# A new order table for the first two batches of an attention and gated-MLP kernel

## The chip, the core and the metric

The kernel runs on one core of a Trainium2 chip. Its engines are named as in the profile: PE multiplies matrices, DVE and POOL work on elements, ACT evaluates functions and copies, and SP issues most of the DMAs. The metric is the time of one execution on the device in microseconds (us). It is not the span: the span is the stretch between the first and the last instruction in the trace, and the time is a little longer.

## What is computed

Eight batches of 576 positions. Windowed attention of 8 heads (half of them with a window of 32 positions, half with every fourth of the last 128) gives x with 512 columns. A gated layer follows, and then a layer that mixes positions:

```python
gate = 1.0 / (1.0 + np.exp(-gate_pre))      # gate_pre: a causal convolution of x, 5 taps
val = x @ w_val
x = gate * val @ w_mid                       # 512 columns
h = np.maximum(x @ w_in, 0.0)                # 1024 columns
u, v = h[..., :512], h[..., 512:]
v_n = (v - mu) / np.sqrt(var + 1e-06)        # over the columns of v
v_s = np.einsum('ts,bsd->btd', w_spatial, v_n) + b_spatial[None, :, None]
out = (u * v_s) @ w_out
```

## The kernel before

The 8 heads of a batch are taken in 4 pairs, numbered 0 to 3; "(1,2)" below is batch 1, pair 2. For each pair the steps are `a_scores` (PE writes `s_ps`), `a_max`, `a_exp`, `a_sum` (the softmax on `e_t`, by DVE, ACT and POOL), `a_trans`, `a_pv` (PE writes `o_ps` from `pt` and `vv_t`, ACT copies it to `xt`), `a_conv` (five products on DVE, into `tt`) and `a_tanh`. In batch 0 `a_trans` goes through PE (`t_ps`). In batches 1 and later DVE transposes into one tile `et`, and SP copies it by 16 small DMAs, `pt<-et`, into the one tile `pt`; `a_pv` of the pair reads `pt`, so the copies of a pair cannot begin before `a_pv` of the pair ahead has read it.

The layers are `val` (`val_ps`), `v` and `norm` (`v_ps`, `v_t`), `u` (`u_ps`), `sp` (`sp_ps`) and `out` (`out_ps`). In place of two products by w_mid and w_in, the kernel first multiplies the two weights: `fuse("wiv", e)` for the columns of v and `fuse("wiu", e)` for those of u (both write `w_ps`). The raw weights arrive as 64-bit floating point; `w_f32` turns them into 32-bit numbers by an ACT and four DVE instructions (`wm_f`, `wiv_f`, `wv_f`, `wiu_f`, `wo_f`). From batch 1 on, and in `v`, `u`, `sp` and `out` always, every operand is split into a high and a low part, and three products replace one: ACT makes the high part (`gh`, `wiu_h`), POOL or DVE the low one (`gl`, `wiu_l`, `wm_l`, `wsp_l`, `w_l`). `val` of batch 0 is done on 32-bit operands unsplit, 32 products in all. The small results on PE share four buffers, which come free when the tile has been evicted; raw pieces of `w_spatial`, of its bias and of `w_out` share four buffers.

What sets the order is a queue. Each step is a key, and each key has one or more numbers (one for each piece of the step); the queue hands out the piece with the smallest number next, and every engine executes its instructions in the order in which the pieces were handed out. All instructions are recorded by one helper, so the profile gives line 635 for each. Batch 3 and later take their numbers from `EVERY`, shifted by 74.5 for each batch; the start takes them from the table `EARLY`:

```python
    def times(key):
        if key in EARLY:
            return EARLY[key]
        name, b, *rest = key
        return [t + PERIOD * (b - START) for t in EVERY[(name, *rest)]]
```

The numbers order the pieces and do nothing else.

Of the kernel before, what the change touches and what calls it, by code (L numbers as in the profile page):

```python
# [61 lines left out]
def _swapped(b, x):  # L62
# [172 lines left out]
    ("a_exp", 0, 3): (33.69,),
    ("load_mask", 3): (33.84,),
    ("a_trans", 0, 2): (34.99, 38.62, 39.08, 39.51, 39.95,),
    ("fuse", "wiv", 1): (35.58, 37.69, 39.20, 40.13, 41.28, 42.34,),
    ("load_vv", 1, 1): (37.97,),
    ("a_tanh", 0, 0): (38.49,),  # L240
    ("a_conv", 0, 1): (39.78, 45.98, 47.46, 51.00, 58.32,),
    ("load_w", "wiu", 0): (39.90,),
    ("a_sum", 0, 3): (40.23, 40.72,),
    ("val", 0, 0, 0): (42.47, 44.17, 44.70, 49.21, 50.01, 50.49, 51.00,),
    ("a_trans", 0, 3): (43.00, 43.58, 43.86, 44.29, 44.73,),
    ("a_conv", 0, 2): (44.10, 45.23, 46.72, 48.20, 56.83,),
    ("load_w", "wiu", 1): (44.23,),
    ("a_max", 1, 0): (44.55, 51.74,),
    ("fuse", "wiv", 2): (45.23, 47.35, 48.28, 49.74, 52.45, 53.58,),
    ("w_f32", "wiu", 0): (46.82, 48.95, 50.38, 52.42, 54.93,),  # L250
    ("a_conv", 0, 3): (49.56, 54.19, 56.09, 57.58, 59.06,),
    ("val", 0, 2, 0): (50.67, 51.21, 51.74, 57.08, 59.80, 61.65, 67.12,),
    ("split_pair", "wm", 0): (50.88, 65.63, 65.63, 69.24,),
    ("w_f32", "wiu", 1): (51.41, 60.98, 62.33, 63.81, 67.47,),
    ("val", 0, 3, 0): (52.27, 52.81, 54.94, 55.48, 61.59, 63.48, 64.28,),
    ("split_pair", "wm", 1): (52.94, 70.03, 70.36, 72.71,),
    ("val", 0, 1, 1): (53.34, 53.87, 54.41, 57.61, 61.96, 63.14, 65.97, 82.59,),
    ("a_exp", 1, 0): (53.46,),
    ("val", 0, 1, 0): (56.01, 56.54, 58.15, 58.68, 66.42, 66.90, 67.89,),
    ("a_tanh", 0, 2): (57.69,),  # L260
    ("split_sp", 4): (58.28, 76.95, 88.17, 92.02, 93.34, 95.12,),
    ("split_pair", "wiu", 0): (58.85, 59.55, 59.95, 62.64,),
    ("a_scores", 1, 1): (59.21,),
    ("split_sp", 0): (59.38, 72.85,),
    ("a_sum", 1, 0): (60.17, 61.13,),
# [21 lines left out]
    ("a_sum", 1, 1): (77.85, 80.09,),
    ("load_w", "wo", 1): (78.93, 95.96,),
    ("split_pair", "wv", 0): (79.55, 87.45, 90.10, 100.85,),
    ("fuse", "wiu", 2): (79.96, 80.71, 81.41, 82.10, 83.00, 83.61,),  # L290
    ("split_sp", 1): (80.11, 81.20,),
    ("load_vv", 1, 2): (80.24,),
    ("a_trans", 1, 1): (81.27, 82.11, 86.50, 89.06, 91.62,),
# [1178 lines left out]
```

## Time and profile before

| | us |
|---|---|
| time, median of 3 runs | 658.89 (658.78 to 660.42) |
| the profiled execution, its own time | 659.71 |
| its span | 657.9 |
| PE busy | 635.6 |
| DVE busy | 455.8 |
| POOL busy | 309.0 |
| ACT busy | 305.1 |

The profiled execution is 0.82 above the median, and 1.81 longer than its span. The granted clock of PE is 1.00 in every stretch. An engine's busy time is the sum over the stretches in which it had an instruction at work, whatever that instruction was held up by inside.

### The profile page before, as it was taken

The page shows a single profiled execution, that of the slowest core. Times are in us where ns is not written, and L with a number is a line of the kernel's source. Part 1 is how long each engine was busy: PE and PEld are TensorE (multiplying, and loading weights), DVE is VectorE, ACT ScalarE, POOL GpSimd, SP SyncE. Part 2 cuts the span into 40 slices and gives each one's busy share as a digit, 9 for nine tenths or more (in the row PEclk, how much of TensorE's full clock was granted, in tenths as well). Part 3 has the DMA queues.
Part 4 walks back from the last instruction along what each step waited for, and adds up shares of the span by engine and source line. Part 5 has one row for each costly group of instructions (what it writes and reads, how often), then busy time and mean ns, then how long its engine had stood idle before and what let it go on. Part 6 is the DMA issues. An engine that isn't in the chain of part 4 may idle for free.

```text
span 657.9 us, 17770 instructions
## 1 busy us (share of the span) xinstructions
PE 635.6 (97%) x7248; PEld 585.6 (89%) x7248; DVE 455.8 (69%) x789; ACT 305.1 (46%) x702; POOL 309.0 (47%) x378
## 2 busy tenths in 40 slices
PE   3889999999999999999999999999999999999998
PEld 2547789999899989999899989999899989999997
DVE  4999688997686588767676688767676688633410
ACT  4887676544443344443444434443444435442422
POOL 1114995746543374435634464435634364524430
PEclk9999999999999999999999999999999999999999
DMA  8971333352133332343123433343123411120002
GB/s 330 417 283 38 112 99 127 91 158 70 40 108 80 86 80 76 79 130 100 31 63 106 121 79 76 80 132 99 31 64 106 120 42 40 20 75 1 1 1 72
DMA packets 85605, 63.58 MB, mean 97 GB/s; under 512 B 64530, under 2 KB 74642, under 8 KB 85012
## 3 DMA queue, kind: packets, MB, share of 16 engines
q1 hardware_dynamic: 76308, 53.01, 28.3%
q10 hardware_dynamic: 9216, 9.44, 4.1%
q8 instruction: 57, 0.93, 0.6%
q14 instruction: 24, 0.20, 0.1%
HBM read 44.92 MB, written 9.44 MB: 83 GB/s over the span
## 4 chain that ended last, share of the span: by engine, by line
PE 80%; DVE 9%; DMA 4%; POOL 3%; ACT 3%; issue 1%; SPq 0%; ACTq 0%; DVEq 0%; POOLq 0%
PE sp_ps L635 17%; PE u_ps L635 14%; PE out_ps L635 14%; PE v_ps L635 14%; PE val_ps L635 13%; PE o_ps L635 4%; PE s_ps L635 3%; DVE tt L635 3%; DMA raw<-in_w_in 2%; DMA raw<-in_w_mid_t 1%; DVE wo_f L635 1%; DVE wiu_f L635 1%; POOL wsp_l L635 1%; ACT pt L635 1%; DMA qk_t<-in_qk 1%
## 5 line engine op out<-in xcount | busy, mean ns | idle before, releaser
L635 DVE SCALAR_TENSOR_TENSOR tt<-xt,cw,tt 128x576 f32<-128x576 f32 x116 | 118.6, 1029 | 1.2
L635 PE MATMUL sp_ps<-wsp_h,vh 128*128 128x288 f32 x320 | 93.7, 297 | 0.0
L635 POOL TENSOR_TENSOR gl<-tt,gh 128x288 fp32r<-128x288 f32 x64 | 61.1, 962 | 49.9 <-ACT gh L635 46.3
L635 POOL TENSOR_TENSOR g2l<-ru,g2h 128x288 fp32r<-128x288 f32 x64 | 55.6, 876 | 52.3 <-ACT g2h L635 52.2
L635 PE MATMUL u_ps<-gh,w_h 128*128 128x288 f32 x256 | 76.4, 298 | 0.0
L635 PE MATMUL out_ps<-g2h,wout_h 128*128 128x288 f32 x256 | 76.2, 298 | 0.0
L635 PE MATMUL out_ps<-g2h,wout_l 128*128 128x288 f32 x256 | 75.5, 295 | 0.2 <-POOL wout_l L635 0.2
L635 PE MATMUL u_ps<-gl,w_h 128*128 128x288 f32 x256 | 75.4, 295 | 0.0
L635 PE MATMUL sp_ps<-wsp_h,vl 128*128 128x288 f32 x256 | 75.4, 295 | 0.0
L635 PE MATMUL u_ps<-gh,w_l 128*128 128x288 f32 x256 | 75.4, 295 | 0.0
L635 PE MATMUL sp_ps<-wsp_l,vh 128*128 128x288 f32 x256 | 75.4, 295 | 0.0
L635 PE MATMUL out_ps<-g2l,wout_h 128*128 128x288 f32 x256 | 75.4, 294 | 0.0
L635 PE MATMUL val_ps<-xh,wval_h 128*128 128x288 f32 x224 | 66.8, 298 | 0.0
L635 PE MATMUL val_ps<-xl,wval_h 128*128 128x288 f32 x224 | 66.1, 295 | 0.7 <-POOL xl L635 0.7
L635 PE MATMUL val_ps<-xh,wval_l 128*128 128x288 f32 x224 | 66.0, 295 | 0.0
L635 POOL TENSOR_TENSOR xl<-xt,xh 128x576 fp32r<-128x576 f32 x28 | 42.5, 1518 | 47.2 <-ACT xh L635 46.0
L635 POOL TENSOR_TENSOR vl<-v_t,vh 128x512 fp32r<-128x512 f32 x32 | 41.9, 1311 | 41.6 <-ACT vh L635 41.6
L635 POOL TENSOR_TENSOR e_t<-e_t,sm 128x576 f32<-128x576 f32 x31 | 38.1, 1229 | 48.9 <-DVE sm L635 22.4
L635 PEld LDWEIGHTS sp_ps<-wsp_h,vh 128*128 128x128 f32 x320 | 60.0, 188 | 0.8
L635 PE MATMUL v_ps<-w_h,gh 128*128 128x512 f32 x160 | 58.8, 392 | 0.6 <-DVE tt L635 0.6
L635 PE MATMUL v_ps<-w_l,gh 128*128 128x512 f32 x160 | 58.5, 390 | 0.0
L635 ACT CAST g2h<-ru 128x288 fp32r<-128x288 f32 x64 | 27.2, 431 | 63.2 <-DVE ru L635 63.0
(127 smaller groups left out, 1644.4 us busy)
## 6 DMA issues: line engine op xcount, KB each, us to landing
qk_t<-in_qk SPq DMA_DIRECT2D x30, 592.0 KB, 4.4
vv_t<-in_vv SPq DMA_DIRECT2D x30, 384.0 KB, 3.6
out<-ob ACTq DMA_DIRECT2D x64, 144.0 KB, 1.8
raw<-in_w_in SPq DMA_DIRECT2D x4, 1024.0 KB, 4.9
pt<-et SPq DMA_DIRECT2D x240, 16.0 KB, 1.9
pt<-et SPq DMA_DIRECT2D x144, 20.0 KB, 2.7
raw<-in_w_mid_t SPq DMA_DIRECT2D x2, 1024.0 KB, 12.5
raw<-in_w_val SPq DMA_DIRECT2D x2, 1024.0 KB, 13.2
```

Of the source, the lines that this page charges most:

```text
L635: ins = self._tc.keep_in_program_order(fn(*args, **kwargs))
```

## The change

All 358 keys of `EARLY` stay, and the numbers up to about 153 are others. Those that follow, from `val` (1,1,1) on, are the same in both tables, and so are `EVERY`, `PERIOD` and `START`. No instruction is added or taken away: PE has the same 5424 matmuls, DVE the same 789 instructions. From the product `v` (1,0) on, the order on PE is the same in both. One key shows what the diff looks like:

```diff
-    ("a_pv", 1, 2): (105.11, 113.93, 115.39,),
+    ("a_pv", 1, 2): (104.156, 107.023, 113.475,),
```

On PE, the end of `val` of batch 0 (`val_ps` from `wv_f`) and the beginning of `fuse` for wiu. Before:

```order
L635 MATMUL val_ps<-xt,wv_f_441 128x288 x2
L635 MATMUL w_ps<-wiv_f_221,wm_f_156 128x512
L635 MATMUL o_ps<-pt,qkv 64x96 x12
L635 MATMUL w_ps<-wiv_f_221,wm_f_156 128x512 x2
L635 MATMUL val_ps<-xt,wv_f_441 128x288
L635 MATMUL w_ps<-wiv_f_221,wm_f_156 128x512
L635 MATMUL val_ps<-xt,wv_f_441 128x288 x16
L635 MATMUL s_ps<-qk_t 32x64 x36
L635 MATMUL val_ps<-xt,wv_f_441 128x288 x12
L635 MATMUL w_ps<-wiu_h,wm_h 128x512
```

And now:

```order
L635 MATMUL w_ps<-wiv_f_205,wm_f_137 128x512 x2
L635 MATMUL val_ps<-xt,wv_f_437 128x288 x2
L635 MATMUL o_ps<-pt,qkv 64x96 x12
L635 MATMUL s_ps<-qk_t 32x64 x36
L635 MATMUL val_ps<-xt,wv_f_437 128x288 x30
L635 MATMUL w_ps<-wiu_h,wm_h 128x512
```

The last four products of `fuse` for wiv and the scores of (1,1) now stand ahead of 30 products of `val` in a row. After them PE has, before, 6 products of wiu's fuse, the scores of (1,2), 12 of `v`, 27 of the fuse, `a_pv` of (1,0) and the last 15 of the fuse; now it has 6 of the fuse, 24 of `v`, 3 of the fuse, the scores of (1,2), `a_pv` of (1,0) and the last 39 of the fuse, and then 32 of `v` and 36 of `u`, the scores and `a_pv` of (1,1).

On SP, the copies of the pairs (1,2) and (1,3); a row with x4 is four issues. Before:

```order
L635 DMA pt<-et 32x192 x4
L635 DMA pt<-et 32x96 x4
L635 DMA pt<-et 32x192 x4
L635 DMA pt<-et 32x96 x4
L635 DMA mask_sb<-in_masks 128x576
L635 DMA qk_t<-in_qk 128x1184
L635 DMA vv_t<-in_vv 128x768
L635 DMA pt<-et 32x192 x4
L635 DMA pt<-et 32x96 x4
L635 DMA pt<-et 32x192 x4
L635 DMA pt<-et 32x96 x4
```

And now:

```order
L635 DMA pt<-et 32x192 x4
L635 DMA vv_t<-in_vv 128x768
L635 DMA pt<-et 32x96 x4
L635 DMA mask_sb<-in_masks 128x576
L635 DMA raw<-in_w_out 128x1024
L635 DMA pt<-et 32x192 x4
L635 DMA raw<-in_w_out 128x1024
L635 DMA pt<-et 32x96 x4
L635 DMA raw<-in_w_out 128x1024
L635 DMA pt<-et 32x192 x4
L635 DMA pt<-et 32x96 x4
```

Loads of `w_out`, of a mask and of `vv_t` now stand among the copies of (1,2), and those of (1,3) follow with one load of `w_out` between. The places of the two `a_pv` on PE have moved too: between `a_pv` of (1,1) and of (1,2) there are now 60 products of `u`, 38 of `sp` and the scores of (1,3), and between those of (1,2) and of (1,3) 72 of `sp`, 6 of `out`, 2 of `sp` and 6 of `out`.

## Rows read from the trace of the kernel before

**Rows 1.** The page: busy time of each engine, share of the span, instructions.

```profile
PE 635.6 (97%) x7248; PEld 585.6 (89%) x7248; DVE 455.8 (69%) x789; ACT 305.1 (46%) x702; POOL 309.0 (47%) x378
```

**Rows 2.** Busy us (instructions) of each engine by stretch, clock, DMA share, GB/s.

```profile
core 0: us, PE busy (x) PEld busy (x) DVE busy (x) ACT busy (x) POOL busy (x), PEclk, DMA share, GB/s
...
50.00:60.00 10.00, 10.00 (x108) 7.33 (x106) 10.00 (x15) 7.69 (x27) 1.40 (x1) 1.00 0.01 2
60.00:70.00 10.00, 8.88 (x104) 6.26 (x102) 9.97 (x16) 5.90 (x14) 9.40 (x7) 1.00 0.25 76
70.00:80.00 10.00, 9.67 (x53) 7.84 (x55) 7.17 (x13) 8.49 (x29) 9.86 (x9) 1.00 0.35 107
...
300.00:374.00 74.00, 74.00 (x890) 70.31 (x889) 52.38 (x95) 31.84 (x62) 35.68 (x47) 1.00 0.34 88
```

**Rows 3.** Waits of PE: for whom, us in total, times, longest.

```profile
PE s_ps L635 <- DMA qk_t<-in_qk: 8.3, 2, 4.9
```

**Rows 4.** Chain that ended last, its end: start, us, what.

```profile
588.99 12.72 PE val_ps L635 x96
601.71 12.72 PE v_ps L635 x56
```

**Rows 5.** PE in time: start, us, operation, count, idle before.

```profile
60.88 6.11 PE L635 MATMUL val_ps<-xt,wv_f 128*128 128x288 f32 x24 [0.85 <-DVE tt L635]
...
83.89 0.39 PE L635 MATMUL w_ps<-wiu_h,wm_l 128*128 128x512 f32 x1
...
107.63 0.98 PE L635 MATMUL s_ps<-qk_t 64*32 64x64 f32 x72 [1.07 <-DVE e_t L635]
...
115.87 1.21 PE L635 MATMUL o_ps<-pt,vv_t 128*64 128x96 f32 x24
...
131.17 1.21 PE L635 MATMUL o_ps<-pt,vv_t 128*64 128x96 f32 x24
```

**Rows 6.** DVE in time, 43 to 65 us: start, us, operation, count.

```profile
43.87 1.22 DVE L635 SCALAR_TENSOR_TENSOR wv_f<-raw,wv_f 128x1024 int32<-128x1024 int32 x1
...
45.00 0.52 DVE L635 TENSOR_SCALAR tt<-xt,cw 128x576 f32<-128x576 f32 x1
...
45.43 0.75 DVE L635 SCALAR_TENSOR_TENSOR e_t<-s_ps,mask_sb 128x576 f32<-128x576 f32 x1
...
46.10 3.73 DVE L635 SCALAR_TENSOR_TENSOR tt<-xt,cw,tt 128x576 f32<-128x576 f32 x5
...
50.77 0.46 DVE L635 SCALAR_TENSOR_TENSOR tt<-tt,val_ps 128x288 f32<-128x288 f32 x1
...
52.47 0.75 DVE L635 TENSOR_REDUCE mx<-e_t 128x9 f32<-128x576 f32 x1
...
54.26 0.69 DVE L635 SCALAR_TENSOR_TENSOR w_l<-w_ps,w_h 128x512 fp32r<-128x512 f32 x1
...
63.90 0.77 DVE L635 STREAM_TRANSPOSE et<-e_t 128x576 f32<-128x576 f32 x1
```

**Rows 7.** DMA issues of SP in time: start, us, count.

```profile
64.73 8.54 SPq L635 DMA_DIRECT2D pt<-et  x12
...
102.94 10.62 SPq L635 DMA_DIRECT2D pt<-et  x16
...
113.66 0.53 SPq L635 DMA_DIRECT2D mask_sb<-in_masks  x1
...
119.12 10.99 SPq L635 DMA_DIRECT2D pt<-et  x16
```

**Rows 8.** DVE and POOL by shape, 0 to 160 us: busy, mean ns, idle before.

```profile
L635 DVE SCALAR_TENSOR_TENSOR tt<-xt,cw,tt 128x576 f32<-128x576 f32 x21 | 18.8, 929 | 0.1
...
L635 DVE SCALAR_TENSOR_TENSOR tt<-tt,val_ps 128x288 f32<-128x288 f32 x15 | 6.6, 448 | 1.7 <-PE val_ps L635 1.7
...
L635 POOL TENSOR_TENSOR gl<-tt,gh 128x288 fp32r<-128x288 f32 x15 | 15.6, 1056 | 12.1 <-ACT gh L635 8.6 <-ACT xt L635 3.6
...
L635 POOL TENSOR_TENSOR wsp_l<-sp_raw,wsp_h 128x576 fp32r<-128x576 f32 x4 | 6.2, 1557 | 0.0
```

More of the change, by code (lines that the diff above doesn't have):

```diff
@@ L237 @@
[L237 to L265, printed above, removed]
@@ L287 @@
[L287 to L293, printed above, removed]
-    ("a_split", 1, 0): (81.34, 103.60,),
-    ("a_max", 1, 2): (82.10, 82.89,),
-    ("a_conv", 1, 1): (82.99, 98.42, 99.87, 102.15, 107.39, 108.75,),
@@ new lines @@
+    ("fuse", "wiv", 1): (11.208, 13.359, 22.199, 22.916, 26.739, 29.368,),
+    ("a_max", 0, 2): (11.447, 11.686,),
+    ("w_f32", "wiv", 1): (12.403, 16.465, 17.182, 17.421, 17.660,),
+    ("load_qk", 0, 3): (12.642,),
+    ("a_pv", 0, 3): (13.120, 36.297, 37.492,),
+    ("a_trans", 0, 1): (13.598, 14.075, 16.704, 18.615, 18.854,),
+    ("load_vv", 0, 0): (13.836,),
+    ("load_w", "wv", 1): (14.314,),
+    ("load_w", "wv", 0): (14.792,),
+    ("load_qk", 1, 0): (15.509,),
+    ("a_scores", 0, 3): (15.748,),
@@ new lines @@
+    ("a_exp", 0, 2): (16.226,),
+    ("fuse", "wiv", 3): (18.376, 20.766, 21.721, 22.677, 24.828, 28.890,),
+    ("w_f32", "wv", 1): (19.332, 28.412, 30.084, 31.518, 38.208,),
+    ("w_f32", "wv", 0): (19.571, 25.306, 25.545, 25.783, 30.323,),
+    ("a_sum", 0, 2): (20.049, 25.067,),
+    ("a_max", 0, 3): (20.288, 20.527,),
+    ("a_exp", 0, 3): (21.244,),
+    ("a_pv", 1, 0): (21.483, 64.014, 67.359,),
+    ("a_pv", 0, 1): (22.438, 23.872, 30.562,),
+    ("load_vv", 0, 1): (23.155,),
+    ("load_vv", 1, 0): (23.633,),
@@ new lines @@
+    ("load_mask", 2): (24.350,),
+    ("load_sp", 0): (26.022,),
+    ("a_sum", 0, 3): (26.261, 29.129,),
+    ("load_vv", 0, 2): (26.500,),
+    ("a_trans", 0, 2): (26.978, 27.695, 29.845, 30.801, 31.040,),
+    ("a_pv", 0, 2): (27.217, 31.757, 32.952,),
+    ("a_scores", 1, 0): (27.456,),
+    ("a_pv", 1, 1): (27.934, 90.536, 91.492,),
+    ("load_vv", 0, 3): (28.173,),
+    ("fuse", "wiv", 2): (28.651, 29.607, 32.235, 32.474, 35.102, 40.837,),
+    ("a_trans", 0, 3): (31.279, 31.996, 32.713, 33.191, 34.863,),
@@ new lines @@
+    ("w_f32", "wiu", 1): (51.828, 61.864, 62.341, 62.580, 64.253,),
+    ("split_pair", "wiu", 0): (52.306, 53.740, 55.412, 59.713,),
+    ("a_tanh", 0, 3): (53.023,),
+    ("a_max", 1, 1): (53.979, 59.952,),
+    ("val", 0, 3, 1): (54.695, 55.890, 56.368, 57.324, 58.757, 60.430, 76.678, 79.784,),
+    ("fuse", "wiu", 1): (57.563, 69.032, 70.704, 73.094, 77.395, 84.802,),
+    ("load_qk", 1, 2): (57.802,),
+    ("split_sp", 4): (58.518, 72.855, 80.740, 100.811, 102.006, 102.483,),
+    ("fuse", "wiu", 0): (59.235, 66.403, 70.226, 77.156, 77.634, 77.873,),
@@ new lines @@
+    ("out", 1, 1, 1): (213.790, 217.230, 220.810,),
+    ("val", 2, 0, 1): (215.390, 216.590, 217.180, 219.000, 219.510, 221.030,),
+    ("out", 1, 3, 1): (216.990, 220.000, 220.430,),
+    ("a_tanh", 2, 3): (218.410,),
+    ("a_pv", 3, 1): (218.450, 246.880, 247.320, 248.200, 249.900,),
+    ("a_scores", 3, 2): (218.980,),
+    ("val", 2, 0, 0): (220.030, 221.280, 221.880, 222.360, 222.870,),
+    ("val", 2, 1, 0): (221.680, 225.490, 226.380, 226.860, 227.370,),
+    ("val", 2, 2, 1): (222.880, 225.030, 226.750, 227.230, 228.270, 236.750,),
@@ L533 @@
+    ("a_split", 3, 3): (287.890, 288.640,),
+    ("out", 2, 3, 1): (289.080, 294.450, 294.880,),
+    ("a_tanh", 3, 3): (293.480,),
 }
```

602 lines of the change are left out of this document (293 added, 309 removed), and 19 rows, old and new, of the table EARLY.

## The prediction

> **What bounds the kernel now.** The busy times come first: PE works 635.6 us of a span of 657.9 [rows 1], so it idles 22 us in all. The stretches then say where. In a batch in the middle, 300 to 374 us, PE is busy 74.00 of 74 us [rows 2]: nothing is to be had there, and the changed table does not reach it. At the start PE waits 8.3 us for `qk_t` alone [rows 3], while the first inputs arrive; the new table loads that tile first as well. From about 14 us on DVE has no gap (10.00 of 10 us from 50 to 60, 9.97 from 60 to 70) and gets one only near 75 (7.17 from 70 to 80), while POOL goes from 1.40 to 9.40 and 9.86 [rows 2]. So up to some 75 us the order of DVE's work decides when PE can begin a product, and behind that PE itself is the bound, apart from single gaps such as the 1.07 us before the scores at 107.63 [rows 5].
>
> The orders on PE are equal from `v` (1,0) on. If PE has finished everything ahead of that product x us earlier, and nothing else is late, the whole rest moves up by x, because the rest is PE at work without gaps. So I look for x alone.
>
> For the walk I need PE's pace at work: 96 products of `val_ps` took 12.72 us, which is 0.1325 each (`u`, `sp` and `out` have the same shape), and 56 of `v_ps` 12.72, which is 0.227 each [rows 4]; those of wiu's fuse have the same 512 columns. A call of scores takes 0.98, an `a_pv` 1.21. A `val` product of batch 0 has two records, so the 24 records in 6.11 us are 12 products of 0.51 [rows 5].
>
> **The change part by part.** It adds and removes no instruction; each term below is a shift.
>
> *First, `val` of batch 0.* Its long row needs the fourth `wv_f`, which ended at 45.09 (43.87 + 1.22). In the new order DVE has more ahead of it: three convolution products (3 of the five that took 3.73, so 2.2), one eviction of scores (0.75), one maximum (0.75) and one scaling (0.52) [rows 6]. That is 4.2 us, so it ends at 49.3. What PE had between its pieces of `val` before is then done, and the row starts there. PE has four small buffers, so the fifth `val` tile, nine products later, waits until DVE has evicted the first one. Between that `wv_f` and that eviction DVE has six convolution products (4.5), one scaling (0.52), one `w_l` (0.69), one scaling of `wiu_f` (taken as long as that) and the eviction itself (0.46) [rows 6]: 6.9, so 56.2. Seventeen products are left: 17 x 0.49 to 0.51 is 8.3 to 8.7, and `val` ends at about 64.7. Before, it ended at 66.99 (60.88 + 6.11). That is 2.3 us earlier.
>
> *Second, wiu's fuse and `a_pv` of (1,0).* Behind `val` PE now has 6 + 24 + 3 products of 0.227 (7.5) and one call of scores (0.98), so it comes to `a_pv` (1,0) at 73.2. The copies `pt<-et` of that pair wait for DVE's transpose, which ended at 64.67 (63.90 + 0.77) [rows 6]. Summing the durations of all that stands ahead of it on DVE in either order gives 3.3 us less now: 61.4. Twelve copies took 8.54 us, 0.71 each [rows 7], so sixteen take 11.4, and a load of `qk_t` among them, taken as a mask's 0.53 [rows 7], makes it 73.3. From the end of the last copy's issue to `a_pv` it took 2.3 us in (1,2) (102.94 + 10.62 = 113.56; 115.87) and 1.06 in (1,3) (119.12 + 10.99 = 130.11; 131.17) [rows 5, 7]. So `a_pv` starts at 74.4 to 75.6, a wait of 1.2 to 2.4 that was not there before. Then 1.21 for it and 39 x 0.227 = 8.85: the fuse ends at 84.5 to 85.7. Before, it ended at 84.28 (83.89 + 0.39) [rows 5], but with 12 products of `v` fewer done, which are 2.7 us. With those it would have ended at 87.0, so the new order is ahead by 1.3 to 2.5. Against this stand the low parts: the last `wm_l` is 3.2 us further back in DVE's order, and the last `wiu_h` on ACT stands behind the copy of `a_pv` (1,0). I allow 0.9 for them at the low end: 0.4 to 2.5, and take 1.8, nearer to the bare walk, since the fuse's other products (27 of the 39) can run ahead of the last chunk's.
>
> *Third, the gap at 107.63.* The scores of (2,0) waited there until DVE had evicted those of (1,3) from the one tile `s_ps` (1.07 us [rows 5]). In the new order two `a_pv` and 86 products stand between these two calls, 2 x 1.21 + 11.4 = 13.8 us, in which DVE can do that eviction; I take +1.1, with 0 as the other bound.
>
> *Fourth, `a_pv` of (1,2) and (1,3).* `pt` is one tile, so a pair's copies begin after the `a_pv` ahead. Between (1,1) and (1,2) PE has 98 products of 0.1325 and one call of scores, 14.0 us. The copies need 10.6 to 11.0, the four loads among them some 2.1 (each as the mask's 0.53), and 1.06 to 2.3 pass from the last issue to `a_pv` [rows 5, 7]: 13.8 to 15.4, a wait of 0 to 1.4. Between (1,2) and (1,3) PE has 86 products, 11.4 us; the copies need 11.7 to 13.3, a wait of 0.3 to 1.9. Before, (1,3) came 14.1 us after (1,2) had ended (115.87 + 1.21; 131.17), and PE had work for all of it. Together 0.3 to 3.3; I take 1.5, a little under the middle.
>
> *The sum:* 1.8 + 1.1 - 1.5 = 1.4 us earlier, with 0.4 + 0 - 3.3 = -2.9 and 2.5 + 1.1 - 0.3 = +3.3 as bounds. The profiled execution took 659.71 (1.81 of it outside the span) and would take 658.3; the median stands 0.82 lower, so the time I give is **657.5**.
>
> [...] A convolution product, two inputs in SBUF, takes 0.75 us in a row of five at 46.10, when POOL is nearly idle, and 0.929 on average up to 160 us; an eviction of a `val` tile, one input in PSUM, takes 0.46 and 0.448, POOL busy or not [rows 6, 8]. [...]
>
> **The rivals.**
>
> *The copies take all of it (no change).* With both waits of the fourth term at their upper ends the sum is 1.8 + 1.1 - 3.3 = -0.4: 659.3. For it: 16 issues took 10.6 us or more in both rows of SP [rows 7]. Against it: only 1.06 us passed from the last issue to `a_pv` in the later one.
>
> *Slower: a load in front of the copies of (1,1).* On SP the fifth load into the four raw buffers now stands right before the copies of (1,1), and its buffer comes free when POOL has made a `wsp_l` (1.557 us [rows 8]), the fifteenth piece of POOL's work since its first `gl`. POOL's work ahead of it depends on ACT's last `wiu_h`, behind `a_pv` (1,0); by sums it ends near 82. Then 16 copies (10.6), two loads (1.1) and 1.06 to 2.3: 94.8 to 96.0. PE comes to `a_pv` (1,1) at about 98.1 (the fuse's end at 85.1, 32 x 0.227, 36 x 0.1325, 0.98). The slack is 2 to 3 us. It decides from the point where that `wsp_l` ends after 85; at 90 the wait is some 5 us, and the sum 1.4 - 5 = -3.6: 662.5. For it: POOL was busy 9.40 and 9.86 of 10 us there [rows 2]. Against it: the slack.
>
> [...]
>
> *More than the sum.* If the fuse loses nothing at all, the waits of the fourth term stay at their lower ends, and DVE meets less of POOL from 75 to 150 us, the gain is the upper bound of the sum or a little more, 3.3 to 4.2: 654.7 to 655.6. For it: PE still idles 1.5 us between 60 and 80 [rows 2]. Against it: it needs all three.
>
> **How the numbers follow.** What a measurement of this kernel tells from no change is about 0.3%, 2 us: faster is under 656.9, slower over 660.9. Chances: the sum as forecast (655.6 to 658.6) 0.45; more than that 0.17; the copies take it 0.12; POOL under the convolution 0.09; slower by the load or another such wait 0.17. Faster holds the second case and half of the first, 0.40; slower is the last, 0.17; same is the rest, 0.43. The likeliest case's own range is 655.6 to 658.6. For eight in ten I go from 654.5, the end of the larger gain, to 661.4, which leaves most of the last case out.
>
> **What would show it.** `val` of batch 0 ends near 64.7 in place of 66.99; PE waits 1 to 2 us before `a_pv` (1,0) and the fuse ends near 85 with 24 products of `v` done; no gap before the scores of (2,0); waits of about 0.4 and 1.1 before `a_pv` of (1,2) and (1,3); `v` (1,0) 1.4 us earlier. A wait before `a_pv` (1,1), a `val` row that ends after 66, or a wait of several us at a fuse would make the prediction wrong.

## The result, and the profile after

The changed kernel takes 663.17 us (median of 17 runs, 660.26 to 666.81), the kernel before 659.23 (17 runs beside them, 657.66 to 661.12). The ratio is 1.0058, 95% interval 1.0041 to 1.0075: slower by 0.58%. The prediction gave 657.5, most likely the same or faster, with a range up to 661.4; the time lies above it. The profiled execution took 666.81, the longest of the 17, 7.10 over that of before (659.71), so its waits and its clock are those of a long execution: its mean granted clock is 0.992, that of the median execution 0.995.

By the page, the span is 665.0 us, 7.1 more than before. PE is busy 2.3 us longer for the same work [rows 1] and stands still for 27.1 us, 4.8 more:

```profile
PE 637.9 (96%) x7248; PEld 590.1 (89%) x7248; DVE 456.8 (69%) x789; ACT 304.2 (46%) x702; POOL 307.4 (46%) x378
```

By stretches (columns as in [rows 2]):

```profile
30.00:40.00 10.00, 10.00 (x52) 4.67 (x56) 9.24 (x16) 6.52 (x23) 1.39 (x4) 0.83 0.46 176
60.00:70.00 10.00, 10.00 (x44) 7.96 (x43) 9.68 (x15) 7.40 (x20) 7.82 (x8) 1.00 0.28 79
70.00:80.00 10.00, 9.64 (x128) 7.72 (x127) 8.83 (x15) 5.97 (x19) 7.73 (x7) 1.00 0.06 14
...
110.00:120.00 10.00, 5.82 (x114) 5.09 (x112) 4.71 (x9) 5.01 (x21) 6.09 (x7) 1.00 0.54 159
...
150.00:160.00 10.00, 7.99 (x90) 7.64 (x88) 5.13 (x11) 0.73 (x2) 2.31 (x2) 1.00 0.34 93
160.00:170.00 10.00, 8.68 (x38) 8.19 (x39) 8.39 (x16) 4.92 (x11) 8.06 (x13) 0.66 0.40 92
...
300.00:374.00 74.00, 74.00 (x890) 70.32 (x890) 53.95 (x96) 31.72 (x62) 35.87 (x46) 1.00 0.30 80
```

From 60 to 70 us PE now has no gap (8.88 before [rows 2]); in its place it is busy 5.82 of 10 from 110 to 120 and 7.99 from 150 to 160. Two stretches have a granted clock under 1 (the first columns are the stretch, its length and PE's busy time, the third number from the end is the clock), where before had 1.00 throughout:

```profile
30.00:34.00 4.00, 4.00 (x6) 1.70 (x7) 3.77 (x7) 0.52 (x2) 1.23 (x3) 0.57 0.99 374
161.00:165.00 4.00, 3.68 (x15) 3.68 (x16) 2.56 (x7) 2.40 (x6) 3.23 (x8) 0.50 0.37 99
165.00:170.00 5.00, 5.00 (x25) 4.51 (x24) 4.83 (x9) 1.79 (x4) 4.84 (x6) 0.83 0.49 101
```

Read in windows of half a us, the clock is 0.50 from 30.5 to 33.5 us and from 160.0 to 166.5, and 1.00 in the others from 28 to 43 and from 160 to 175, save the three in which it changes (0.71, 0.88 and 0.76); so the stretches with a value between hold some of either. In PE's timeline (start, us, operation, idle before) there is a long idle stretch at each, of 2.46 and of 3.33 us; the clock falls 0.3 us behind the end of the first and 2.0 us into the second:

```profile
29.89 8.83 PE L635 MATMUL w_ps<-wiv_f,wm_f 128*128 128x512 f32 x16 [2.46 <-DVE wiv_f L635]
...
51.79 14.82 PE L635 MATMUL val_ps<-xt,wv_f 128*128 128x288 f32 x60
...
76.34 0.68 PE L635 MATMUL o_ps<-pt,vv_t 128*64 128x96 f32 x10 [0.36 <-DMA pt<-et]
...
85.74 0.39 PE L635 MATMUL w_ps<-wiu_h,wm_l 128*128 128x512 f32 x1
...
98.07 1.03 PE L635 MATMUL s_ps<-qk_t 64*32 64x64 f32 x72
99.03 1.41 PE L635 MATMUL o_ps<-pt,vv_t 128*64 128x96 f32 x24
...
113.53 0.40 PE L635 MATMUL sp_ps<-wsp_h,vh 128*128 128x288 f32 x1 [1.77 <-ACT ru L635]
...
115.58 0.97 PE L635 MATMUL s_ps<-qk_t 64*32 64x64 f32 x72
117.19 0.91 PE L635 MATMUL o_ps<-pt,vv_t 128*64 128x96 f32 x12 [0.64 <-DMA pt<-et]
119.87 0.84 PE L635 MATMUL o_ps<-pt,vv_t 128*64 128x96 f32 x12 [1.76 <-DMA pt<-et]
...
161.32 0.61 PE L635 MATMUL val_ps<-xh,wval_h 128*128 128x288 f32 x1 [3.33 <-DVE tt L635]
...
166.53 0.49 PE L635 MATMUL v_ps<-w_h,gh 128*128 128x512 f32 x1
```

These answer to [rows 5]. `val` of batch 0 ends at 66.61 (51.79 + 14.82; before 66.99), the fuse of wiu at 86.13 (85.74 + 0.39). The scores of (1,3) start at 98.07, right ahead of `a_pv` (1,1), and those of (2,0) at 115.58, without a gap; the call that the section on the change names between the two `a_pv` is that of (2,0). Ahead of it comes a wait of 1.77 us for ACT's `ru`, behind it both halves of `a_pv` (1,2) wait for the copies (0.64 and 1.76), and at `val` of batch 1 PE waits 3.33 us for DVE. That last place, shortly ahead of the point from which the two tables are equal, is called the join below. `v` (1,0) starts at 166.53; before it started at 158.52:

```profile
158.52 0.40 PE L635 MATMUL v_ps<-w_h,gh 128*128 128x512 f32 x1
```

To see where these 8.0 us arise although the orders on PE differ, I subtract from the start of a product the time of all PE work ahead of it at full pace (0.1325 for a `val`, 0.227 for a `v` as in [rows 4], 0.49 for a `val` of batch 0, and so on). What is left is the time that PE has lost so far: idle, at a lower clock, or in rows next to a stop (the first product behind the 1.77 us took 0.40 where the next ones took 0.29 or 0.30). The columns are points with equal work done.

| PE's lost us | at wiu's fuse | after 85 us of work | after 105 | after 127 | at `v` (1,0) | end |
|---|---|---|---|---|---|---|
| before | 21.65 | 25.27 | 25.66 | 26.99 | 27.01 | 33.90 |
| after | 21.17 | 22.77 | 28.46 | 29.11 | 35.02 | 40.97 |

So the new order was ahead as forecast, by 2.5 us after 85 us of work, and lost 5.7 by 105 (4.17 of it the three idle stretches from 111 to 120) and 5.9 by `v` (1,0). The second loss is 3.33 of idle time and 2.4 of clock: 21 products in 5.21 us (161.32 to 166.53) in place of 21 x 0.1325 = 2.8.

On SP, the copies of (1,2) (answering to [rows 7]):

```profile
100.25 0.33 SPq L635 DMA_DIRECT2D raw<-in_w_out  x1
100.63 1.43 SPq L635 DMA_DIRECT2D qk_t<-in_qk  x2
102.16 3.49 SPq L635 DMA_DIRECT2D pt<-et  x4
105.70 0.70 SPq L635 DMA_DIRECT2D vv_t<-in_vv  x1
106.44 4.22 SPq L635 DMA_DIRECT2D pt<-et  x4
110.77 1.20 SPq L635 DMA_DIRECT2D mask_sb<-in_masks  x1
112.07 0.38 SPq L635 DMA_DIRECT2D raw<-in_w_out  x1
112.50 2.42 SPq L635 DMA_DIRECT2D pt<-et  x4
115.02 0.53 SPq L635 DMA_DIRECT2D raw<-in_w_out  x1
115.59 2.42 SPq L635 DMA_DIRECT2D pt<-et  x4
```

They take 15.85 us (102.16 to 118.01), where [rows 7] has 10.62. The four loads among them are 2.8 of it; the first eight copies take 0.87 and 1.06 each, the last eight 0.60. On DVE this is handed on, since `et` and `pt` are single tiles and DVE works in order. Before, the transpose of (1,3) came without a wait:

```profile
118.32 0.77 DVE L635 STREAM_TRANSPOSE et<-e_t 128x576 f32<-128x576 f32 x1
```

And now:

```profile
103.59 3.96 DVE L635 TENSOR_SCALAR v_t<-v_t,mv,rs 128x512 f32<-128x512 f32 x1
...
120.27 0.78 DVE L635 STREAM_TRANSPOSE et<-e_t 128x576 f32<-128x576 f32 x1 [5.40 <-DMA pt<-et]
...
149.65 0.81 DVE L635 SCALAR_TENSOR_TENSOR tt<-tt,val_ps 128x288 f32<-128x288 f32 x2
...
156.95 0.78 DVE L635 STREAM_TRANSPOSE et<-e_t 128x576 f32<-128x576 f32 x1 [4.70 <-DMA pt<-et]
...
160.82 0.81 DVE L635 SCALAR_TENSOR_TENSOR tt<-tt,val_ps 128x288 f32<-128x288 f32 x2
```

The transpose of (1,3), at 120.27, waits 5.40 us, that of (2,1), at 156.95, 4.70, with evictions of `val` tiles behind it in the queue; PE's 3.33 us end with the first of them, at 160.82.

### The profile page after: what moved, and what is told of

Same layout as the page of the kernel before. It is cut to its first block, busy times and chain, and to the rows that moved or that the text cites. A ratio compares the mean times of both kernels' runs of the same rounds, so it can differ in the third digit from the quotient of the medians.

```text
span 665.0 us, 17772 instructions
## 1 busy us (share of the span) xinstructions
PE 637.9 (96%) x7248; PEld 590.1 (89%) x7248; DVE 456.8 (69%) x789; ACT 304.2 (46%) x702; POOL 307.4 (46%) x378
## 4 chain that ended last, share of the span: by engine, by line
PE 82%; DVE 8%; ACT 3%; DMA 3%; SPq 1%; issue 1%; POOL 1%; DVEq 0%; POOLq 0%; ACTq 0%
PE sp_ps L635 16%; PE out_ps L635 15%; PE val_ps L635 14%; PE u_ps L635 14%; PE v_ps L635 13%; PE o_ps L635 4%; PE s_ps L635 3%; PE w_ps L635 2%; DMA pt<-et 1%; SPq L635 1%; DVE wm_f L635 1%; DMA raw<-in_w_mid_t 1%; DVE wiv_f L635 1%; DVE wo_f L635 1%; DVE tt L635 1%
## 5 line engine op out<-in xcount | busy, mean ns | idle before, releaser
L635 DVE SCALAR_TENSOR_TENSOR tt<-xt,cw,tt 128x576 f32<-128x576 f32 x116 | 116.9, 1011 | 1.4
L635 POOL TENSOR_TENSOR gl<-tt,gh 128x288 fp32r<-128x288 f32 x64 | 59.4, 934 | 46.8 <-ACT gh L635 46.7
```

Source lines behind the costliest of these rows:

```text
L635: ins = self._tc.keep_in_program_order(fn(*args, **kwargs))
```

## Experiments

Every edit moves pieces in the queue's order, and no instruction is added or taken away. Each median is beside runs of the kernel before on the same chip, and the ratio is to them. "After" is the changed kernel. Three theories are tested. A: PE's start is really earlier, and the loss comes from about 100 us on, from loads among the copies and the single `et` and `pt`. B: DVE is held up by POOL there. C: the idle stretch at 27 us and the lower clock behind it make the loss. One execution of each kernel was profiled; the waits below are of that one.

**Two halves.** e1, e7 and e8 begin in after's order and go on in before's; e2 begins in before's and goes on in after's. The place where the two orders meet is called the seam.

```diff
 e1: after's order up to the last copy of (1,1)
 e7: after's order up to the fifth val tile of batch 0
 e8: as e7, with the edit of e5
-    then after's order
+    then the rest in before's order
 e2: before's order up to the last copy of (1,1)
-    then before's order
+    then the rest in after's order
```

> The new order up to the last copy of pair (1,1) into pt, and behind it the old order of whatever is left. All theories agree on the profile up to 90 us: as in the changed kernel, some 1 us ahead of the old one at the end of wiu's fuse. Theory A (the loss is made by the copies of (1,2) and what stands among them on SP, from 100 us on, and is handed on through the tile et to DVE at the join): not slower than before, 657 to 659.5. Theory B (DVE is held up by POOL from 100 us on, as in the 3.96 us scaling of v_t): the same, since that part is the old one. Theory C (the loss is made at the start, by the idle PE at 27 us and the lower clock after it): slower than before by 2 us or more, 661 to 663.

Measured: 671.61, ratio 1.0185 (1.0172 to 1.0198). PE waits 4.9 us ahead of an `a_pv` and 3.96 ahead of scores; neither wait is in before or in after. The seam makes them, so e1 says nothing of the front half.

> The counterpart: the old order up to the last copy of pair (1,1), and behind it the new order of whatever is left. Theories A and B: most of the loss is there, 661 to 664. Theory C: no loss, 658 to 660.

Measured: 661.13, ratio 1.0023 (1.0013 to 1.0034). Behind before's front, after's tail costs 0.23%, perhaps less: in the profiled execution 1.4 of the 2.2 us that PE is behind at `v` (1,0) are lost ahead of wiu's fuse, where the order is before's (an idle stretch of 1.72 us at 34 us, and a granted clock of 0.76 from 34 to 40). The only new wait is 2.66 us of `val` for DVE at the join. The copies of (1,2) have the same kinds of loads among them, but take 12.5 us, and `a_pv` (1,2) does not wait: there PE comes later, the first loads of `w_out` were issued at 81 and 88.5 us, and fewer loads stand right ahead.

> The new order up to the fifth val tile of batch 0, and behind it the old order of whatever is left: the cut lies ahead of everything that the copies of batch 1 depend on. If the new start is worth what its profile shows, 0.5 us at the end of val, with the lower clock in it, the time is that of before or up to 1 us less: 658 to 659.5. If the first cut's loss was in the start, it is slower by 2 us or more.

> The same with the two products of the fuse moved as in the run for the start. If the lower clock at 30 us costs what the products' length says (1.4 us), this is 1 to 2 us faster than before, 657 to 658.5, and the best so far; if the clock matters to nothing, it is the same as the run without it.

Measured: 661.88, ratio 1.0043 (1.0031 to 1.0056), and 661.35, ratio 1.0033 (1.0022 to 1.0044). Both have one large wait, 4.07 us for DVE's `wm_l` at about 71 us, again from the seam, with a clock of 0.50 in e7 and 0.72 in e8 from 70 to 76 us (several products behind the wait take 0.63 us, those from 77 us on 0.39 or 0.40), and no other over 0.6 from there to `v` (1,0): e7's lost time grows from 28.35 once that is over to 30.72 at `v` (1,0), with before's order. The front half alone could not be told apart from its seam. Nor does the pair price the clock at the start: there e7 has 1.96 us of idle time and the full clock, and e8, which was to mend it, 2.00 us and the lower clock.

**One part undone.** e3 puts DVE's transpose of (2,1), and four that follow it, behind a convolution product and two evictions of `val`; e4 takes loads out from among the copies; e5 moves two products of wiv's fuse (two records each); e6 moves POOL's work off the stretch from 104 to 117.

```diff
 e3, DVE
-L635 STREAM_TRANSPOSE et<-e_t 128x9x2x32
 L635 SCALAR_TENSOR_TENSOR tt<-tt,val_ps 128x288 x2
+L635 STREAM_TRANSPOSE et<-e_t 128x9x2x32
 e4, SP
-L635 DMA qk_t<-in_qk 128x1184 x2
 L635 DMA pt<-et 32x192 x4
+L635 DMA pt<-et 32x96 x4
+L635 DMA pt<-et 32x192 x4
+L635 DMA pt<-et 32x96 x4
 L635 DMA vv_t<-in_vv 128x768
+L635 DMA raw<-in_w_out 128x1024 x3
+L635 DMA qk_t<-in_qk 128x1184
 e5, PE
-L635 MATMUL w_ps<-wiv_f_205,wm_f_137 128x512 x4
+L635 MATMUL w_ps<-wiv_f_205,wm_f_137 128x512 x2
 ...
-L635 MATMUL w_ps<-wiv_f_205,wm_f_137 128x512 x8
+L635 MATMUL w_ps<-wiv_f_205,wm_f_137 128x512 x10
 e6, POOL
+L635 TENSOR_TENSOR e_t<-e_t,sm 128x576
 L635 TENSOR_TENSOR wval_l<-wv_f_437,wval_h 128x512 x2
-L635 TENSOR_TENSOR e_t<-e_t,sm 128x576
 L635 TENSOR_TENSOR xl<-xt,xh 128x576 x2
```

> The changed kernel with one step moved on DVE: the transpose of pair (2,1) and the four steps that need the tile it frees (the scores of (2,2) out of PSUM, their maximum, difference and exponential) stand behind the last product of the convolution of (1,3) and the evictions of two val tiles. Nothing else moves. If the transpose, which waits for the copies out of et, holds up PE at the join (theory A's last step), the wait of 3.3 us of val at 158 us and the lower clock behind it go: 3 to 5 us less than the changed kernel, 658 to 660. If val waits for something else there, no change: 662 to 664.

Measured: 665.9, ratio 1.0099 (1.0084 to 1.0113). The wait of `val` is gone, and one of `v_ps` stands in its place (who waits, for whom, us in total, times, longest):

```profile
PE v_ps L635 <- DVE tt L635: 3.7, 1, 3.7
```

> The changed kernel with the loads moved on SP: the first qk_t of batch 2 goes ahead, to behind the copies of (1,1); the second qk_t, vv_t of (1,3), three pieces of w_out and a mask go from among the copies of (1,2) to behind them. Two pieces of w_out's conversion follow their loads on ACT. Theory A: the copies of (1,2), 15.9 us from the first to the last issue, take 11 to 12, a_pv of (1,2) waits 2 us or more less, and the copies of (2,0) and the transpose of (2,1) come earlier by the same: 658 to 661. Theory B: the scaling of v_t still takes 4 us, DVE is as late, 662 to 664.

Measured: 661.83, ratio 1.0032 (1.0018 to 1.0046). The copies of (1,2) now run without a break, and `a_pv` (1,2) does not wait:

```profile
99.45 10.26 SPq L635 DMA_DIRECT2D pt<-et  x16
```

This is 0.64 a copy, and the ratio falls from 1.0058 to 1.0032, a difference that the two intervals just bear out. But `ru` (1.9), `a_pv` of (1,3) (1.1) and the join (2.3) still wait.

> The changed kernel with two products of wiv's fuse moved on PE: the second chunk's first two wait until the scores of (0,3) are done, so that PE has 1.85 us of work in the stretch at 27 us in which it idled 2.46 us for wiv_f. Nothing else moves. Theory C (the idle PE and the lower clock behind it, 0.83 from 30 to 40 us, cost 1 to 2 us at the start): the granted clock stays 1.00, the second half of the fuse takes 7.4 us in place of 8.8, and the time falls by 1 to 2 us, to 661 to 662. Theory A alone: the copies are as late whatever PE does before, within 0.5 us of the changed kernel.

Measured: 664.62, ratio 1.0076 (1.0064 to 1.0088). At the start the profiled execution does what it should:

```profile
29.03 7.13 PE L635 MATMUL w_ps<-wiv_f,wm_f 128*128 128x512 f32 x16 [1.04 <-DVE wiv_f L635]
```

The idle time falls from 2.46 to 1.04 us, the clock stays at 1.00, and the 16 records take 7.13 in place of 8.83. PE is 4.6 us ahead of before after 85 us of work (20.68 lost) and 0.7 behind after 105 (26.37). At wiu's fuse it was 2.9 ahead. The gain is gone 20 us of work later, with the same waits as in after, the lower clock at the join among them (0.66 from 156 to 166 us). Theory C fails: the start is mended, and the time is no shorter.

> The changed kernel with four of POOL's pieces moved behind the softmax product of (1,3): two wval_l and the two xl that take over their buffer. They are the pieces during which a scaling of v_t on DVE took 3.96 us. Theory B (DVE held up by POOL sets the end there): the scaling falls to 0.5 to 2 us, PE's wait of 1.8 us for ru at 112 us goes, and the time falls by 1.5 us or more, to 661.5 or less. Theory A (the copies of (1,2) set the end): ru's wait shrinks, but a_pv of (1,2) waits for the copies by as much more, and the time stays within 0.7 us of the changed kernel.

Measured: 665.95, ratio 1.009 (1.007 to 1.0109). The wait for `ru` is gone, so POOL's work in that stretch made it; `a_pv` (1,2) waits 2.58 and 1.09 instead. Theory B names a true wait, but taking it away wins nothing.

**Several parts undone together.** e9 mends the join further (the transpose of (2,1) also behind `xt`), e10 is e4 and e5, e11 is e10 with e6 and an earlier softmax sum of (2,0), e12 is e11 with e9.

```diff
 e9, DVE
-L635 STREAM_TRANSPOSE et<-e_t 128x9x2x32
 L635 SCALAR_TENSOR_TENSOR tt<-tt,val_ps 128x288 x2
 L635 TENSOR_TENSOR xt<-o_ps,xt 128x4x96
+L635 STREAM_TRANSPOSE et<-e_t 128x9x2x32
```

> The changed kernel with the join mended in one more step than the earlier run did: the transpose of (2,1) and its four followers stand behind the evictions of two val tiles and behind DVE's part of a_pv (2,0), and POOL's two clearings of xt for it stand ahead of two gl. If the wait at the join is only the place of these pieces on DVE, PE's waits at 158 to 165 us shrink to 1 us or less and the clock stays at 1.00: 4 to 6 us less than the changed kernel in its profile, about 659 to 660.5. If the join is late because the copies of (2,0) and (2,1) are late, the wait moves once more, to a_pv (2,1) near 172 us or to v (1,0): 662 to 666.

> The changed kernel with both the fuse's two products moved (as in the run for the start) and the loads moved (as in the run for the loads). Theory A: the start alone gave nothing because the copies of (1,2) held the end; with these mended its 2 to 3 us reach further, and the time falls by more than the loads alone gave: 659 to 661. If the join loses whatever comes, it stays at 661.5 to 663.

> The same and two more: POOL's four pieces moved as in the run for POOL (ru's wait at 112 us), and the softmax sums of (2,0) on DVE and POOL moved ahead of two pieces of w_out's conversion, so that the transpose of (2,0), which came 4.7 us later than before at 139 us, comes earlier. Theory A: the copies of (2,0) begin at 134 us or earlier (139.9 in the changed kernel, 135.2 before), the wait at the join is below 1.5 us, and the time is 656.5 to 659.

> The same and the mended join. If the join's wait is a matter of order on DVE alone, 0.5 to 2 us less than the run without it; if the copies set it, the copies of (2,1) now begin later than they need and it is 0 to 2 us more.

Measured: e9 664.28, ratio 1.0069 (1.0047 to 1.0092); e10 660.61, 1.0032 (1.0019 to 1.0045); e11 662.66, 1.0056 (1.0044 to 1.0068); e12 665.18, 1.009 (1.0077 to 1.0103). e9's wait goes to `v_ps` (2.5 us), and so does e12's. e10 has the ratio of e4 alone. In its profile the start was not mended, although the edit of e5 is in it:

```profile
29.32 8.83 PE L635 MATMUL w_ps<-wiv_f,wm_f 128*128 128x512 f32 x16 [2.02 <-DVE wiv_f L635]
```

e11 has 4.9 us less lost than before after 85 us of work, and then waits 2.10 for DVE's `ru`, 0.84 for `wout_l`, 1.21 for ACT's `ob` and 1.51 at the join, with a clock of 0.76 from 124 to 131 us: nothing is left.

**The opposite, and the late `w_out`.** e13 puts loads among the copies in the kernel before. In after, e14 splits `w_spatial` earlier, which frees the raw buffers, so that all four loads of `w_out` go ahead of the copies of (1,2). e15 is e14 and e5.

```diff
 e13, SP, against before
+L635 DMA qk_t<-in_qk 128x1184 x2
 L635 DMA pt<-et 32x192 x4
 L635 DMA pt<-et 32x96 x4
+L635 DMA vv_t<-in_vv 128x768
+L635 DMA raw<-in_w_out 128x1024
 L635 DMA pt<-et 32x192 x4
+L635 DMA mask_sb<-in_masks 128x576
+L635 DMA raw<-in_w_out 128x1024
 L635 DMA pt<-et 32x96 x4
 e14, SP, against after
+L635 DMA raw<-in_w_out 128x1024 x2
 L635 DMA qk_t<-in_qk 128x1184
+L635 DMA raw<-in_w_out 128x1024 x2
 ...
-L635 DMA raw<-in_w_out 128x1024
 L635 DMA pt<-et 32x192 x4
-L635 DMA raw<-in_w_out 128x1024
 L635 DMA pt<-et 32x96 x4
-L635 DMA raw<-in_w_out 128x1024
```

> The kernel before with one edit, the opposite of e4: two loads of qk_t go ahead of the copies of (1,2), and a load of vv_t, two of w_out and one of a mask among them; nothing else is moved. Theory A (loads ahead of and among these copies cost PE time, because et and pt are single tiles): a_pv of (1,2) waits about 2 to 4 us where it did not wait before, and the time is 1.5 to 4 us over that of before (ratio 1.002 to 1.006). Rival (the copies have slack, and the loss comes from the order of DVE's and POOL's work): under 1 us at a_pv of (1,2), ratio within 1.0015 of 1.

Measured: 667.97, ratio 1.0135 (1.0118 to 1.0152). `a_pv` (1,2) waits 7.0 us, where theory A gave 2 to 4:

```profile
PE o_ps L635 <- DMA mask_sb<-in_masks: 5.2, 1, 5.2
PE o_ps L635 <- DMA pt<-et: 1.8, 1, 1.8
```

On SP, ahead of the copies:

```profile
96.24 12.89 SPq L635 DMA_DIRECT2D qk_t<-in_qk  x2
```

This row says why: the second `qk_t` held SP until 109.13, just after the scores of (2,0) at 107.81, which free its buffer (from 95 us on SP waits 11.9 us for `s_ps`), so the copies began 6.3 us later than in [rows 7]. The direction holds, that what stands ahead of and among these copies is paid by PE; the size is mostly the wait for that buffer, and not the issue of loads. So e13 does not show what loads among the copies cost by themselves.

> The changed kernel with the splitting of w_spatial (ACT's wsp_h, POOL's wsp_l) some 40 pieces earlier, so that the raw buffers come free sooner, and the four loads of w_out ahead of the copies of (1,2) in place of one ahead and three among them. Theory A (late w_out loads among the copies are the root): the copies of (1,2) take under 12 us, the scaling of v_t is not held 4 us by POOL, a_pv of (1,2) and (1,3) wait under 1 us together, and the time falls by 2 to 3 us from the 663.2 of the changed kernel. Rival (the loads then block SP ahead of the copies, waiting for their buffers): the copies of (1,2) begin 2 us or more later, a_pv waits as long or longer, and nothing is won.

> The edit of e14 and that of e5 (two products of wiv's fuse behind the scores of (0,3), which took the long idle stretch at 27 us away) together on the changed kernel. Theory A: the 3 us that e5 won at the start are kept as far as about 125 us, the wait at the join (val_ps, some 2 to 3 us) stays, and the time is 658 to 661, at or a little over that of before. Rival (each won us turns into a wait on the next late piece, whatever the order of the loads): 661 to 664, with new waits of 2 us or more between 100 and 130 us.

Measured: 663.75, ratio 1.0069 (1.0051 to 1.0087), and 664.0, ratio 1.0071 (1.0048 to 1.0094). In both, `a_pv` (1,2) waits only 0.25 us, and between 85 and 105 us of work 2.6 and 2.55 us are lost in place of 5.7. The time does not fall: two new waits for POOL stand at 87 and 93 us, and the join still waits, 3.29 us in e14 and 2.14 in e15. In e15's profile the start is not mended either (2.03 us idle and the lower clock). The waits of e14:

```profile
PE val_ps L635 <- DVE tt L635: 3.3, 1, 3.3
...
PE v_ps L635 <- POOL gh L635: 1.1, 1, 1.1
PE v_ps L635 <- POOL gl L635: 1.1, 1, 1.1
```

Theory A's claim that these loads are the root of the loss fails here; that they make the waits of `a_pv` holds.

**The join.** e16 moves the softmax sums of (2,0) ahead of an eviction on DVE and of three pieces on POOL, and one load of `qk_t` behind four copies; e17 is e14 with it, e18 is e15 with it.

```diff
 e16, POOL
+L635 TENSOR_TENSOR e_t<-e_t,sm 128x576
 L635 TENSOR_TENSOR wout_l<-wo_f_1532,wout_h 128x512
 L635 TENSOR_TENSOR g2l<-ru,g2h 128x288
 L635 MEMSET pt 128x1152
 L635 TENSOR_TENSOR wout_l<-wo_f_1670,wout_h 128x512
-L635 TENSOR_TENSOR e_t<-e_t,sm 128x576
```

> The changed kernel with the softmax sums of (2,0) a few pieces earlier on DVE and on POOL (one low part of w_out and three evictions stood ahead of them), and one load of qk_t behind two more of the copies of (2,0). Theory A (the wait of val at the join of the tables is the tail of the single et and pt: the copies of (2,0) run 5 us later than before, so the transpose of (2,1) holds DVE): those copies begin up to 3 us earlier, the 3.3 us wait of val shrinks to under 2 us, and the time falls by 1 to 2.5 us from the 663.2 of the changed kernel. Rival (the wait of val is not set by these copies, or turns into a wait of v_ps as in e9): val and v_ps wait 2.5 us or more together, and the time stays within 1 us.

> The edits of e14 and e16 together. Theory A: e14 left only the wait at the join and two waits on POOL at 87 and 93 us of the execution; with the copies of (2,0) earlier the wait of val (3.29 us in e14) shrinks to under 1.5 us and PE's clock stays at full speed behind it, so the time is 659.5 to 661.5. Rival: the wait moves to v_ps, 662.5 or more.

> The edits of e15 and e16 together: the start of e5, the early w_out path, the early softmax of (2,0). Theory A (the changed order has a better start and loses it all in the pieces between 85 and 165 us): nothing but waits under 1.2 us is left behind 80 us, and the time is 657.5 to 660, at that of before or under it. Rival (each won us turns into a wait on the next late piece): 661.5 or more, with a wait of 2 us or more between 85 and 170 us.

Measured: 663.01, ratio 1.0057 (1.0035 to 1.0079); 663.3, ratio 1.0068 (1.005 to 1.0086); 662.24, ratio 1.0051 (1.0038 to 1.0064). The wait of `val` for DVE falls to 0.5 us in e16 and to nothing in the other two, and new ones stand ahead of it, here in e18's timeline:

```profile
134.57 0.48 PE L635 MATMUL out_ps<-g2h,wout_l 128*128 128x288 f32 x1 [1.60 <-POOL wout_l L635]
...
145.33 0.40 PE L635 MATMUL out_ps<-g2h,wout_h 128*128 128x288 f32 x1 [1.68 <-ACT ob L635]
```

The low part of `w_out` that now follows the softmax on POOL is late. Behind the first of these the clock is under 1.00 too (0.66 from 134 to 139 us; the products take 0.45 us up to 137.7 and 0.29 or 0.30 from 138.2 on). In e16 the copies of (2,0) began only 0.7 us earlier than in after (139.24 against 139.92), so theory A's way to the gain is not what happened: PE came later to the same place. The times are those that the rival gives in e16 to e18, though no wait in e18 reaches its 2 us.

PE's lost time in the runs that tell most, as in the table above:

| PE's lost us | at wiu's fuse | after 85 us of work | after 105 | after 127 | at `v` (1,0) |
|---|---|---|---|---|---|
| before | 21.65 | 25.27 | 25.66 | 26.99 | 27.01 |
| e2, after's tail | 23.05 | 25.26 | 25.76 | 26.30 | 29.23 |
| after | 21.17 | 22.77 | 28.46 | 29.11 | 35.02 |
| e4, loads moved | 20.52 | 21.47 | 25.68 | 26.20 | 28.84 |
| e5, start | 18.76 | 20.68 | 26.37 | 27.00 | 32.75 |
| e11, four parts | 18.89 | 20.40 | 24.77 | 28.21 | 30.00 |
| e14, `w_out` | 20.48 | 24.74 | 27.32 | 27.93 | 33.81 |
| e18, three parts | 18.95 | 23.36 | 26.19 | 31.91 | 32.11 |

The first column spreads over 4.3 us. Whatever PE has won by its 85th us of work, by the 105th it has 24.8 to 28.5 us lost, where before has 25.66. Between there and `v` (1,0) before loses 1.35 us more, and every order with after's tail 3.2 to 6.6.

## Why the prediction was wrong

**The step that failed** is that behind 75 us "PE itself is the bound, apart from single gaps", so that between wiu's fuse and `v` (1,0) the sum needed a term for the two `a_pv` alone. The runs show in its place 1.77 us of waiting for `ru`, and at the join 3.33 us for DVE and 2.4 of clock, 7.5 us that the sum has at nothing. With the terms that it did have, as measured, they come close to the result: 0.9 ahead at the fuse and 1.07 for the gap, less 2.40 at `a_pv` (1,2) and less these 7.5, is 7.9 us behind, where 8.0 were measured; smaller stops are left out.

I read PE as the bound from its busy share. But before has other engines as full in single stretches:

```profile
100.00:110.00 10.00, 8.93 (x133) 8.63 (x132) 9.85 (x16) 4.72 (x11) 7.33 (x8) 1.00 0.41 149
130.00:140.00 10.00, 9.57 (x150) 8.75 (x149) 9.74 (x14) 4.25 (x8) 8.46 (x7) 1.00 0.55 148
```

DVE is busy 9.85 and 9.74 of 10 us there, and the copies fill SP [rows 7]. A full DVE is not the whole of it: where PE waits in after, DVE is busy 4.71 (110 to 120) and 5.13 (150 to 160), and waits itself, 5.40 and 4.70 us, for the copies out of `et`. It is this chain through single tiles that a busy share does not show. e5 shows best that a PE that is ahead waits: 4.6 us ahead, then 0.7 behind. I looked for what the edit delays at four named places, and not at DVE's and POOL's order between 100 and 160 us as a whole.

**First, `val` of batch 0: mis-sized in the profiled run.** It ended at 66.61 and not at 64.7, past the 66 that the prediction named as a sign of being wrong. The walk on DVE was not the fault: in e5, e11 and e18, with the full clock at the start, wiu's fuse begins at 63.8 to 64.0 us (in after at 66.23). What the sum lacked is the idle time of 2.46 us at 27 us and the lower clock behind it (8.83 for 7.13).

**Second, the fuse: right, a half of the size.** It ended at 86.13 with 12 more products of `v` done; before would have been at 87.0. That is 0.9 ahead, where I took 1.8, and the range was 0.4 to 2.5. `a_pv` (1,0) waited 0.36 and not 1.2 to 2.4, since PE came to it at 75.04 and not at 73.2; the copies were issued by 73.56, as forecast (73.3). So two misses cancel in part here, the late `val` and the wait that it hid.

**Third, the gap before the scores of (2,0): right.** It is gone. The working counted between the wrong two calls, though: between the scores of (1,3), at 98.07, and those of (2,0) stand one `a_pv` and 98 products, 14.2 us at full pace, and not two and 86, 13.8.

**Fourth, the copies: right in kind, wrong in place.** `a_pv` (1,2) waited 2.4 us in two halves, not 0 to 1.4, and (1,3) not at all, not 0.3 to 1.9; that the two together lie within 0.3 to 3.3 is in part luck. A load was taken as 0.53 and a copy as 0.66 to 0.69; the loads were 0.38 to 1.20 and eight copies 0.87 to 1.06, and a load of `w_out` and two of `qk_t` stood ahead of the first copy. The wait for `ru` lies in the 14.0 us that this term counts as PE's work without a stop; the join lies behind its last `a_pv`, in a stretch for which the sum has no term.

**The rivals.** "The copies take all of it" named a true wait and gave it more than it took, 3.3 us for 2.4; the rest of the loss is elsewhere. The load ahead of the copies of (1,1) did not delay them: they began at 83.51, and `a_pv` (1,1) at 99.03 had no wait. "Slower" had 0.17, for that load "or another such wait"; it was other such waits. POOL was at work in it, though not under the convolution, which had 0.09: no run shows what that costs, and up to 160 us a convolution product took 0.809 us on average in after, 0.929 before [rows 8]. Before, a scaling of `v_t` with POOL idle took 0.54 us:

```profile
108.56 0.54 DVE L635 TENSOR_SCALAR v_t<-v_t,mv,rs 128x512 f32<-128x512 f32 x1
```

In after, the one at 103.59 took 3.96 us, while POOL had these:

```profile
103.34 1.45 POOL L635 TENSOR_TENSOR wsp_l<-sp_raw,wsp_h 128x576 fp32r<-128x576 f32 x1
104.75 2.52 POOL L635 TENSOR_TENSOR wval_l<-wv_f,wval_h 128x512 fp32r<-128x512 f32 x2
```

It ended at 107.55, 0.28 after POOL's third piece (107.27). How POOL's work could hold a DVE instruction is not shown. e6 moved the two `wval_l` (and two `xl`), and the wait for `ru` was gone.

**What is shown and what stays open.** Shown: the place of the loss; that the loads ahead of and among the copies make the wait of `a_pv` (1,2) (e4, e14); that POOL's pieces make the wait for `ru` (e6); that after's tail behind before's front costs no more than some 0.23% (e2); that PE is up to 4.6 us ahead with a mended start and loses it again (e5); that a wait taken away comes back elsewhere (e3, e6, e9, e12, e14 to e18). Not shown: one cause. No order with after's tail reached before's median, the best being e2 at 1.0023.

How much of the 0.58% is the clock was not measured by itself, but the record bounds it, since it has the mean granted clock of every execution. Of the 72 executions of before beside e1 to e18, 71 have 0.999 or 1.000. The 17 of after have 0.990 to 0.999, with a median of 0.995. The five of them at 0.997 or more have a median time of 661.28, the three at 0.992 or less take 665.29 to 666.81. So the spread of after's times goes largely with the clock. In the profiled execution (0.992) 1.7 and 2.4 us of PE's work time are lost to it, 4.1 of the 7.1. An estimate for the median execution, from its clock: 0.005 of 661 us is some 3.3 us, of the 3.94 between the medians, and less where PE was idle at the lower clock. The five at 0.997 or more are still 2.05 over before, so the clock is not all of it. What an execution of after without the lower clock would take is not shown: at each fall named here there is an idle stretch, which costs its own time.

## What to carry to other kernels

That an engine is busy 97% of the span does not make it the bound in every stretch: before a gain at the start is carried to the end, look in each later stretch for a second engine with 9 of 10 us busy, and for single tiles (`et` and `pt` here) that hand one wait to the next. Where a table sets the order of five engines, a better start needs the later pieces moved with it, and each wait that is removed should be followed to the next that comes up. The cost of small DMAs (0.60 to 1.06 us a copy here) is to be taken from a stretch with the same neighbours on the queue. And an idle stretch of PE can cost twice, by itself (3.33 us at the join) and by a lower clock (2.4 us there), so the granted clock of every execution belongs beside its time.

## What had not been expected of the hardware

In after, PE's idle stretches of 2.46 us at 27 us and of 3.33 at 158 go with a granted clock of 0.50, from 30.5 to 33.5 us and from 160.0 to 166.5. With the order of after or of e5 at the start, the clock fell in all eight profiled executions with 2.37 or 2.46 us idle there (0.83 to 0.86 from 30 to 40 us in the six where that was read; the 16 records of the fuse took 8.70 or 8.83 us in the seven where they were); of the four with 2.00 to 2.10 us it fell in three (e8, e10, e15: 0.83 to 0.85, 8.83 us) and not in one (e1, 2.10: 1.00 from 30 to 34); in the five with 1.04 to 1.96 it did not (e5, e7, e11, e12, e18: 1.00, 7.13 us). Elsewhere it fell behind 1.72 us (e2 at 34 us: 0.76 from 34 to 40) and 1.60 (e18 at 133: 0.66 from 134 to 139), and stayed at 1.00 behind 2.66 (e2 at 155) and 1.75 and 1.98 (e16 at 111 and 117). So the length of an idle stretch alone does not tell.

The issue of one `pt<-et` on SP took 0.60 us in some rows and up to 1.06 in others: the sixteen of (1,2) took 12.55 us in after, the loads left out, and 10.26 in e4. The slow ones stood behind two loads of `qk_t` and one of `w_out`. That the DMA engines were busier does not explain it: their share was 0.84 and 0.61 while a copy took 0.87 and 1.06, and 0.94 and 0.73 while it took 0.60. The reason stays open.

One DVE instruction ended only behind three of POOL's in a row (3.96 us for 0.54).
